# A reordered start in a fused attention and adapter kernel: VectorE only sums, idle matmuls, and a second group of queries loaded as fp32

## The chip, the cores and the metric

The kernel runs on one core of a Trainium2 chip. The core has five engines with instruction queues of their own: TensorE (PE: matmuls and transposes, with weight loads shown apart as PEld), VectorE (DVE), ScalarE (ACT), GpSimd (POOL) and SyncE (SP, which here only issues transfers). Sixteen DMA engines move data for all of them. An engine works through its queue in order, so an instruction that waits holds up all that stands behind it. The metric is the device time of one execution in microseconds (us), as a median over several runs; the profile comes from one execution by itself.

## The reference, cut to what matters

Two parts are fused. The first is attention with pooled keys: `kv` is averaged over 4x4 patches and multiplied by `w_sr`, and the result serves as keys and as values. The second is a mixture of small adapters on the attention's output, of which each row uses the best two of eight.

```python
# q: (4, 12288, 128), kv: (4, 384, 32, 128), w_sr: (128, 128), all fp32
kv_pool = kv.reshape(B, H // 4, 4, W // 4, 4, C).mean(axis=(2, 4))
k = v = kv_pool.reshape(B, -1, C) @ w_sr               # 768 keys per batch
s = (1 / sqrt(C)) * (q @ k.transpose(0, 2, 1))
s = s - s.max(-1, keepdims=True)
a = np.exp(s)
a /= a.sum(-1, keepdims=True) + 1e-09
x = (a @ v).reshape(B * N, C)                          # 49152 rows
logits = x @ w_gate                                    # 8 experts, rank 16 each
# the two largest logits of a row are kept, w = softmax over these two
out = x + sum over the two of w * ((x @ A[e]) @ B[e])
```

## The kernel before

The 49152 query rows are cut into 96 chunks of 512 (`NTOK`), 24 chunks to a batch, four chunks to a group of 2048 rows (`GROWS`, `GRP`). A batch has 768 keys, in six blocks of 128 (`NJ`), two blocks to one of three key tiles (`NT`). The order in which each engine gets its instructions is written out by hand, so the source is the order.

For a chunk `c` the work is: `scores(c, r)` (L231 to L240) for r = 0, 1, 2: two matmuls of a key tile's two blocks with the 512 queries into one of two PSUM buffers `sg`, and one exponential on ACT into `tt`, 1024 values per partition. `weigh(c, h)` (L242 to L251) for two halves: 12 matmuls each, with a piece of `tt` as weights and the values `vext` streaming, into the one buffer of `ps_x`. The values carry eight more columns for the gate's logits and one of ones for the softmax sum. `normalise(c)` (L253 to L267) on DVE: a reciprocal, a multiplication that frees `ps_x`, and four searches of the largest logits. `gate` and `gate_weights` on POOL, ACT and a little DVE, once for two chunks; `transposed` and its copy; `down`, `apply_gate`, `up` and `give` for the adapters, in chunks some iterations behind.

The main loop (L457 to L501) runs over c = 1 to 94. Iteration c computes scores for chunks c + 1 and c + 2, weighs and normalises chunk c - 1, transposes chunk c - 2, goes down with c - 3 and up with c - 6. From a list `todo` it takes three pieces of scores at set places of the iteration. The next batch's keys are prepared inside the loop by `prep` (L202 to L221): its `kv` tiles are loaded at k = 2, 6, 10 and summed on POOL at k = 5 to 15, where k is the chunk's place in its batch.

Queries reach `qT` (channels on partitions, bf16, one tile per group, three buffers) in two ways. Group 0 is loaded as fp32 into `q0` (L93, L97, four rows of 128 values for each of four chunks and each partition) and transposed on PE, in the first part of the program. Every other group goes through memory twice: `cast_q(g)` (L89 to L91) has POOL issue a transfer that turns 2048 rows into bf16 in `q_bf`, and `load_q(g)` (L227 to L229) has SP issue a transposing transfer from there.

The part ahead of the loop (L415 to L452) is what the change is about. SP loads the first batch's key tile 0, then `q0`, then key tiles 1 and 2, each in four transfers of 512 KB. For each key tile t, DVE adds four rows and then eight columns to pool (`sum_row`, L140, three of 1024 values, and `sum_cols`, L144 and L145); `tile_keys(t)` (L176 to L186) transposes the two blocks on PE into `ps_t`, copies them to `kpT` on DVE, multiplies by `w_sr` and copies to `kfT` on ACT; `tile_values(t)` (L188 to L194) makes the values, with the copy on ACT. `queries(h)` (L417 to L424) transposes two chunks of `q0` through `ps_x`, with the copies on ACT. Scores of chunks 0, 1 and 2 are put between. When the second rows of key tile 2 have landed, a small copy `tick` on POOL (L441) lets POOL issue the casts of groups 1, 2 and 3. `load_q(1)` and `load_q(2)` follow on SP.

`ps_x`, `ps_t` and `ps_h` hold one PSUM buffer each, `ps_s` two; `ttpool` has four buffers for `tt`. `mtile` takes the buffer of `ps_h`. `ranges(b)` (L196 to L200) are two DVE reductions over a batch's values for a check at the end.

The loop's lines for the scores and the weighing:

```python
        todo = [(c + 1, 2), (c + 2, 0), (c + 2, 1)]
        ...
        next_scores()
        if c >= 3 and c % 2 == 1:
            gate_weights((c - 3) // 2, nc.gpsimd)
        weigh(c - 1, 0)
        next_scores()
        ...
        weigh(c - 1, 1)
        normalise(c - 1)
```

Of the kernel before, what the change touches and what calls it, by code (L numbers as in the profile page):

```python
# [10 lines left out]
FP32 = mybir.dt.float32  # L11
BF16 = mybir.dt.bfloat16
# [9 lines left out]
def kernel(  # L22
# [10 lines left out]
    nc = tc.nc  # L33
# [55 lines left out]
    def cast_q(g):  # L89
        r = slice(g * GROWS, (g + 1) * GROWS)  # L90
        nc.gpsimd.dma_start(q_bf[r], qflat[r])  # L91

    q0 = kvpool.tile([P, GROWS // NTOK, NS, C], FP32, tag="kvt", name="q0")  # L93
    for t in range(NT):
        load_kv(0, t)
        if t == 0:
            nc.sync.dma_start(q0, qflat[0:GROWS].rearrange("(k s p) c -> p k s c", p=P, s=NS))  # L97

    w_in = const.tile([P, P], FP32)
    nc.scalar.dma_start(w_in, w_sr)  # L100
# [72 lines left out]
        nc.vector.tensor_copy(  # L173
            vext[b][:, :, 0:C + E].rearrange("p (h g) e -> p h g e", h=2), v)

    def tile_keys(t):  # L176

        k = slice(2 * t * P, 2 * (t + 1) * P)
        kp_ps = ps_t.tile([P, 2 * P], FP32, tag="tp", name="kp_ps")
        for u in range(2):  # L180
            mm(kp_ps[:, u * P:(u + 1) * P], kvt[0, t][:, 0, u, 0:C], id_f32, is_transpose=True,
               start=(u == 0), stop=(u == 1), skip_group_check=True)
        nc.vector.tensor_copy(kpT[0][:, k], kp_ps)
        k_ps = mtile([P, 2 * P], name="k_ps")
        mm(k_ps, w_sr_sb, kpT[0][:, k], start=True, stop=True)
        nc.scalar.activation(kfT[0][:, k], k_ps, AF.Copy)  # L186

    def tile_values(t):  # L188
        v_ps = mtile([P, 2, C + E], name="v_ps")
        for g in range(2):  # L190
            j = 2 * t + g
            mm(v_ps[:, g], kpT[0][:, j * P:(j + 1) * P], wext, start=(g == 0), stop=(g == 1),
               skip_group_check=True)
        nc.scalar.activation(vext[0][:, 2 * t:2 * t + 2, 0:C + E], v_ps, AF.Copy)  # L194

    def ranges(b):  # L196
        nc.vector.tensor_reduce(vmax[:, b:b + 1], vext[b][:, :, 0:C], axis=AX.XY,
# [33 lines left out]
    def scores(c, r):  # L231
        b = c // CPB
        if r == 0:
            tt[c] = ttpool.tile([P, NJ, NTOK], F16, tag="tt", name="tt")
        qc = qT[c // GRP][:, (c % GRP) * NTOK:(c % GRP + 1) * NTOK]
        sg = stile("sg")
        for k in range(2):
            j = 2 * r + k
            mm(sg[:, k], kfT[b][:, j * P:(j + 1) * P], qc, start=True, stop=True)  # L239
        nc.scalar.activation(tt[c][:, 2 * r:2 * r + 2], sg, AF.Exp, bias=0.0, scale=scale)  # L240

    def weigh(c, h):  # L242
        b = c // CPB
        if h == 0:
            xps[c] = ps_x.tile([P, 2, 512], FP32, tag="x", name="xps")
        for j in range(h * NH, (h + 1) * NH):
            for s in range(NS):
                o = xps[c][:, s // 2, (s % 2) * VW:(s % 2 + 1) * VW]
                mm(o, tt[c][:, j, s::NS], vext[b][:, j],  # L249
                   start=(j == 0 and s % 2 == 0), stop=(j == NJ - 1 and s % 2 == 1),  # L250
                   skip_group_check=True)  # L251

# [161 lines left out]

    qT[0] = qpool.tile([P, GROWS], BF16, tag="qT", name="qT")  # L415

    def queries(h):  # L417
        t = ps_x.tile([P, 2, NTOK], FP32, tag="x", name="q_ps")
        for u in range(2):
            k = 2 * h + u  # L420
            for i in range(NS):
                mm(t[:, u, i * P:(i + 1) * P], q0[:, k, i], id_f32, is_transpose=True,
                   start=(i == 0), stop=(i == NS - 1), skip_group_check=True)
            nc.scalar.activation(qT[0][:, k * NTOK:(k + 1) * NTOK], t[:, u], AF.Copy)  # L424

    a_bf = const.tile([P, P], BF16)
    b_half = const.tile([P, P], FP32)
    b_bf = const.tile([P, P], BF16)
    for t in range(NT):
        for d in range(1, 4):  # L430
            sum_row(0, t, d, nc.vector)
        sum_cols(0, t, nc.vector)
        tile_keys(t)
        if t == 0:
            nc.vector.tensor_copy(a_bf, a_f)
            nc.vector.tensor_scalar(b_half, b_f, 0.5, None, op0=ALU.mult)
            nc.vector.tensor_copy(b_bf, b_half)
            queries(0)
        if t == NT - 1:
            tick = const.tile([P, 1], FP32)  # L440
            nc.gpsimd.tensor_copy(tick, kvt[0, t][:, 1, 0, 0:1])  # L441
            for g in range(1, 4):
                cast_q(g)
        scores(0, t)
        tile_values(t)
        if t == 0:
            queries(1)
        scores(1, t)
        if t < NT - 1:
            scores(2, t)  # L450
    load_q(1)
    load_q(2)  # L452


# [2 lines left out]
    for c in range(1, NCH - 1):  # L457
        b, k = divmod(c, CPB)
        todo = [(c + 1, 2), (c + 2, 0), (c + 2, 1)]

        def next_scores():
            x, r = todo.pop(0)
            if x < NCH:
                scores(x, r)

        cs = c + 2
        if cs < NCH and cs % GRP == 0:
# [3 lines left out]
            if g + 3 < NQ:  # L471
                cast_q(g + 3)
        next_scores()
        if c >= 3 and c % 2 == 1:
            gate_weights((c - 3) // 2, nc.gpsimd)
        weigh(c - 1, 0)
        next_scores()
        if chunk_ok(c - 6):
            up(c - 6)
            give(c - 6)  # L480
        weigh(c - 1, 1)
        normalise(c - 1)
# [195 lines left out]
```

## Time and profile before

| What | us |
|---|---|
| median of three runs | 412.86 |
| lowest and highest of them | 411.19, 413.30 |
| the profiled execution | 412.09 |
| its span, first to last instruction | 410.3 |
| PE busy in the span | 380.0 (93%) |
| DVE busy | 344.4 (84%) |
| ACT busy | 297.9 (73%) |
| POOL busy | 165.2 (40%) |
| mean granted clock of PE | 0.991 |

The page's second part cuts the span into 40 equal slices of 10.26 us; each digit is an engine's busy share of a slice in tenths, 9 for 90% or more:

```profile
PE   0659999999999999999999999989999999999992
PEld 0426888777877888877877888867878788787791
DVE  3663789898899989898899989898898989899982
ACT  1267888876687877876687878866777888877751
POOL 1020498882212487792212488692212212122120
```

PE is busy almost throughout from the fourth slice on, which is the main loop. The first three slices, some 31 us, are the part ahead of the loop, where it is not. The last slice is the end of the work. A chunk's turn in the loop can be read from the start times of its reciprocal on DVE (L256), of which there are 96: the first at 36.1, the last at 395.0.

In the timeline a row gives the start and the duration of a group of like instructions, the engine, the line, the operation, what it writes and reads with partitions and elements, how many there are, and in brackets how long the engine had been idle before, and what ended that. In the windows view a row is a stretch of time with each engine's busy time in it, the clock granted to PE (PEclk, 1.00 is full), the busy share of the DMA engines and what they moved.

### The profile page before, as it was taken

Reading aid. Unit: us, or ns where it says so; the run is one execution under the profiler, and the core shown is the slowest. Engines: PE = TensorE matmul, PEld = TensorE weight load, DVE = VectorE, ACT = ScalarE, POOL = GpSimd, SP = SyncE. Lnnn points to the kernel's source line nnn. Section 1 sums busy time; section 2 is a strip of 40 time slices with the busy share of each in tenths; the row PEclk is TensorE's granted clock in tenths of the full one; section 3 lists DMA queues with packets and bytes.
Section 4 is the critical chain, followed back from the end, with each engine's and each line's share of the span. In section 5 each row is a group of like instructions: output and inputs, shape, how many; then the busy total and the mean of one; then the engine's idle time right before and its main releaser. Section 6 shows DMA issues by size and latency. Waiting matters only on the chain.

```text
span 410.3 us, 11470 instructions
## 1 busy us (share of the span) xinstructions
PE 380.0 (93%) x4561; PEld 304.0 (74%) x4561; DVE 344.4 (84%) x969; ACT 297.9 (73%) x356; POOL 165.2 (40%) x315
## 2 busy tenths in 40 slices
PE   0659999999999999999999999989999999999992
PEld 0426888777877888877877888867878788787791
DVE  3663789898899989898899989898898989899982
ACT  1267888876687877876687878866777888877751
POOL 1020498882212487792212488692212212122120
PEclk9998999999999999999999999999999999999998
DMA  8999699797186999797186999797185474221123
GB/s 259 378 251 181 232 248 289 284 185 154 66 169 134 290 244 310 241 249 156 60 173 119 322 233 305 263 227 154 55 180 115 139 162 129 79 78 74 57 80 135
DMA packets 71372, 76.51 MB, mean 186 GB/s; under 512 B 51744, under 2 KB 52000, under 8 KB 70944
## 3 DMA queue, kind: packets, MB, share of 16 engines
q1 hardware_dynamic: 68816, 62.93, 55.1%
q0 software_dynamic: 736, 12.06, 16.8%
q10 hardware_dynamic: 1760, 0.73, 0.7%
q8 instruction: 37, 0.61, 0.6%
q14 instruction: 23, 0.19, 0.1%
HBM read 50.53 MB, written 37.22 MB: 214 GB/s over the span
## 4 chain that ended last, share of the span: by engine, by line
PE 79%; DMA 8%; DVE 7%; issue 2%; ACT 1%; ACTq 0%; SPq 0%; DVEq 0%; POOL 0%
PE xps L249 31%; PE sg L239 26%; PE t_ps L306 9%; PE d_ps L350 5%; PE h_ps L329 4%; DMA qT<-q_bf 3%; DMA b_f<-in_moe_B_dram 3%; DMA kvt<-in_kv_dram 2%; DVE xn L260 2%; DVE hg L334 2%; DMA q_bf<-in_q_dram 1%; PE v_ps L171 1%; PE k_ps L164 1%; DVE osb L358 1%; ACT tt L240 1%
## 5 line engine op out<-in xcount | busy, mean ns | idle before, releaser
L240 ACT ACTIVATE tt<-sg 128x1024 f16<-128x1024 f32 x288 | 282.6, 1022 | 75.8 <-PE sg L239 75.3
L239 PE MATMUL sg<-qT,kfT 128*128 128x512 bf16 x576 | 172.3, 382 | 2.4 <-ACT kfT L186 1.0
L249 PEld LDWEIGHTS <-tt 128*128 128x128 f16 x2304 | 154.6, 113 | 23.7 <-DVE xn L260 2.1
L249 PE MATMUL xps<-vext,tt 128*128 128x137 f16 x2304 | 170.9, 224 | 0.6 <-DVE xn L260 0.4
L358 DVE TENSOR_TENSOR osb<-d_ps,xn 128x512 f32<-128x512 f32 x90 | 62.1, 689 | 17.7 <-PE d_ps L350 14.3
L273 POOL TENSOR_TENSOR m<-top 128x8 f32<-128x8 f32 x47 | 10.9, 232 | 157.5 <-DVE top L267 157.2
L260 DVE TENSOR_TENSOR xn<-xps,rinv_all 128x548 f32<-128x548 f32 x96 | 69.9, 728 | 3.3
L140 POOL TENSOR_TENSOR kvt<-kvt 128x1024 f32<-128x1024 f32 x27 | 64.0, 2372 | 4.3 <-PE sg L239 1.9
L334 DVE TENSOR_TENSOR hg<-h_ps,gw 128x512 bf16<-128x512 f32 x94 | 63.8, 678 | 0.4 <-PE h_ps L329 0.4
L315 DVE COPY xh<-t_ps 128x1024 bf16<-128x1024 bf16 (+1 forms) x93 | 62.4, 671 | 0.0
L239 PEld LDWEIGHTS <-kfT 128*128 128x128 bf16 x576 | 45.3, 98 | 5.7 <-issue 2.3
L350 PEld LDWEIGHTS <-xh 128*128 128x128 bf16 x384 | 29.2, 98 | 25.8 <-issue 5.6
L329 PEld LDWEIGHTS <-xh 128*128 128x128 bf16 x384 | 29.2, 98 | 21.0 <-issue 0.7
L267 DVE MAX8 top<-xn 128x8 f32<-128x8 f32 x384 | 36.0, 156 | 3.3
L350 PE MATMUL d_ps<-b_bf,xh 128*128 128x128 bf16 x360 | 34.8, 219 | 3.2 <-DVE hg L334 2.9
L329 PE MATMUL h_ps<-a_bf,xh 128*128 128x128 bf16 x376 | 36.3, 219 | 0.6 <-DVE cnt L398 0.6
L306 PE MATMUL t_ps<-id_bf,hg 128*128 128x128 bf16 x376 | 36.3, 219 | 0.0
L306 PE MATMUL t_ps<-id_bf,xn 128*128 128x128 bf16 x376 | 36.3, 219 | 0.0
L288 POOL TENSOR_SCALAR th<-th 128x64 f32<-128x64 f32 x47 | 17.4, 370 | 37.4 <-ACT th L286 37.4
L256 DVE RECIPROCAL rinv_all<-xps 128x4 f32<-128x4 f32 x96 | 17.5, 183 | 14.4 <-PE xps L249 11.5
L306 PEld LDWEIGHTS <-xn 128*128 128x128 bf16 x384 | 26.0, 98 | 0.0
L306 PEld LDWEIGHTS <-hg 128*128 128x128 bf16 x384 | 25.4, 98 | 0.1
(96 smaller groups left out, 207.4 us busy)
## 6 DMA issues: line engine op xcount, KB each, us to landing
kvt<-in_kv_dram SPq DMA_DIRECT2D x48, 512.0 KB, 7.2
out_dram<-osb SPq DMA_DIRECT2D x94, 256.0 KB, 3.0
q_bf<-in_q_dram POOLq DMA_DIRECT2D x23, 512.0 KB, 6.3
out_dram<-osb ACTq DMA_DIRECT2D x2, 256.0 KB, 3.7
qT<-q_bf SPq DMA_TRANSPOSE x23, 6.7
w_in<-in_w_sr_dram ACTq DMA_DIRECT2D x1, 64.0 KB, 2.0
a_f<-in_moe_A_dram ACTq DMA_DIRECT2D x1, 64.0 KB, 9.6
b_f<-in_moe_B_dram ACTq DMA_DIRECT2D x1, 64.0 KB, 10.3
```

The source lines that it names most:

```text
L140: eng.tensor_tensor(v[:, 0], v[:, 0], v[:, d], op=ALU.add)
L239: mm(sg[:, k], kfT[b][:, j * P:(j + 1) * P], qc, start=True, stop=True)
L240: nc.scalar.activation(tt[c][:, 2 * r:2 * r + 2], sg, AF.Exp, bias=0.0, scale=scale)
L249: mm(o, tt[c][:, j, s::NS], vext[b][:, j], start=(j == 0 and s % 2 == 0), stop=(j == NJ - 1 and s % 2 == 1), skip_group_check=True)
L260: nc.vector.tensor_tensor(xn[c].rearrange("p (b s) v -> p b s v", b=2), xv, ri.rearrange("p (b s) -> p b s", b=2).unsqueeze(3).broadcast_t ...
L267: nc.vector.max(gin[c // 2][:, (c % 2) * NS + s], xn[c][:, s, C:C + E])
L306: mm(t_ps[:, k, s], src, id_bf, is_transpose=True, start=(i == 0), stop=(i == len(todo) - 1), skip_group_check=True)
L315: nc.vector.tensor_copy(xh[:, lo:hi_], t_ps[:, lo:hi_])
L329: mm(hps[c][:, s], xT[c][:, s], a_bf, start=(s == 0), stop=(s == NS - 1))
L334: nc.vector.tensor_tensor(hg[c].rearrange("p s (e r) -> p (s e) r", r=RK), hps[c].rearrange("p s (e r) -> p (s e) r", r=RK), g.rearrange(" ...
L350: mm(dps[c][:, s], hgT[c][:, s], b_bf, start=(s == 0 and not plus_x), stop=(s == NS - 1), skip_group_check=True)
L358: nc.vector.tensor_tensor(osb, dps[c], xn[c][:, :, 0:C], op=ALU.add)
```

## The change

It touches the part ahead of the loop and the first iterations.

- The second group of queries, rows 2048 to 4095, is loaded as fp32 into a new tile `q1`, by one more SP transfer behind all key loads. `queries_1(k)` transposes chunk 4 + k on PE through `ps_t`, and DVE copies it to `qT[1]`. `cast_q(1)` and `load_q(1)` go.
- In `q0` and `q1` a partition now holds four neighbouring rows of a chunk, 2 KB in one piece, where `q0` had four pieces of 512 bytes. So in the first eight chunks a column block of `tt` is a run of 128 columns, where it was every fourth column, and `weigh` slices accordingly.
- DVE's queue has all sums of the three key tiles first. `kpT` of key tiles 0 and 1 is copied by ACT; the values of key tile 2 are copied by DVE.
- `queries(k)` now does one chunk at a time in half the buffer's size, four calls, put between other work.
- `warm(count)` issues matmuls of the bf16 identity with itself, 128x512 each, into the buffer of `ps_h`; nothing reads them. There are 18 ahead of key tile 0, 8 and 2 around key tile 1, and 2 ahead of key tile 2.
- Chunk 0 is weighed and normalised ahead of the loop, and `scores(3, 0)` is made there; iteration 1 has two pieces of scores left and no weighing.
- `tick` waits for `q1` instead of key tile 2; the casts of groups 2 and 3 follow it.
- `ranges(0)` moves from iteration 1 to iteration 10.

```diff
+    q1 = kvpool.tile([P, GROWS // NTOK, NS, C], FP32, tag="q1", name="q1", bufs=1)
     q0 = kvpool.tile([P, GROWS // NTOK, NS, C], FP32, tag="kvt", name="q0")
     for t in range(NT):
         load_kv(0, t)
         if t == 0:
-            nc.sync.dma_start(q0, qflat[0:GROWS].rearrange("(k s p) c -> p k s c", p=P, s=NS))
+            nc.sync.dma_start(q0, qflat[0:GROWS].rearrange("(k p s) c -> p k s c", p=P, s=NS))
+    nc.sync.dma_start(q1, qflat[GROWS:2 * GROWS].rearrange("(k p s) c -> p k s c", p=P, s=NS))
...
-    def tile_keys(t):
+    def tile_keys(t, between=lambda: None):
...
-        nc.vector.tensor_copy(kpT[0][:, k], kp_ps)
+        if t < NT - 1:
+            nc.scalar.activation(kpT[0][:, k], kp_ps, AF.Copy)
+        else:
+            nc.vector.tensor_copy(kpT[0][:, k], kp_ps)
+        between()
...
-        nc.scalar.activation(vext[0][:, 2 * t:2 * t + 2, 0:C + E], v_ps, AF.Copy)
+        if t < NT - 1:
+            nc.scalar.activation(vext[0][:, 2 * t:2 * t + 2, 0:C + E], v_ps, AF.Copy)
+        else:
+            nc.vector.tensor_copy(vext[0][:, 2 * t:2 * t + 2, 0:C + E], v_ps)
...
-                mm(o, tt[c][:, j, s::NS], vext[b][:, j],
+                rows = slice(s * P, (s + 1) * P) if c < 2 * GRP else slice(s, NTOK, NS)
+                mm(o, tt[c][:, j, rows], vext[b][:, j],
...
-    def queries(h):
-        t = ps_x.tile([P, 2, NTOK], FP32, tag="x", name="q_ps")
-        for u in range(2):
-            k = 2 * h + u
-            for i in range(NS):
-                mm(t[:, u, i * P:(i + 1) * P], q0[:, k, i], id_f32, is_transpose=True,
-                   start=(i == 0), stop=(i == NS - 1), skip_group_check=True)
-            nc.scalar.activation(qT[0][:, k * NTOK:(k + 1) * NTOK], t[:, u], AF.Copy)
+    def queries(k):
+        t = ps_x.tile([P, NTOK], FP32, tag="x", name="q_ps")
+        for i in range(NS):
+            mm(t[:, i * P:(i + 1) * P], q0[:, k, i], id_f32, is_transpose=True,
+               start=(i == 0), stop=(i == NS - 1), skip_group_check=True)
+        nc.scalar.activation(qT[0][:, k * NTOK:(k + 1) * NTOK], t, AF.Copy)
+
+    qT[1] = qpool.tile([P, GROWS], BF16, tag="qT", name="qT")
+
+    def queries_1(k):
+        t = ps_t.tile([P, NTOK], FP32, tag="tp", name="q_ps")
+        for i in range(NS):
+            mm(t[:, i * P:(i + 1) * P], q1[:, k, i], id_f32, is_transpose=True,
+               start=(i == 0), stop=(i == NS - 1), skip_group_check=True)
+        nc.vector.tensor_copy(qT[1][:, k * NTOK:(k + 1) * NTOK], t)
+
+    def warm(count):
+
+        t = mtile([P, NS, P], name="w_ps")
+        for i in range(count):
+            mm(t, id_bf, id_bf.unsqueeze(1).broadcast_to([P, NS, P]), start=True, stop=True)
...
+    tick = const.tile([P, 1], FP32)
+    nc.gpsimd.tensor_copy(tick, q1[:, 0, 0, 0:1])
+    cast_q(2)
+    cast_q(3)
     for t in range(NT):
         for d in range(1, 4):
             sum_row(0, t, d, nc.vector)
         sum_cols(0, t, nc.vector)
-        tile_keys(t)
         if t == 0:
             nc.vector.tensor_copy(a_bf, a_f)
             nc.vector.tensor_scalar(b_half, b_f, 0.5, None, op0=ALU.mult)
             nc.vector.tensor_copy(b_bf, b_half)
-            queries(0)
-        if t == NT - 1:
-            tick = const.tile([P, 1], FP32)
-            nc.gpsimd.tensor_copy(tick, kvt[0, t][:, 1, 0, 0:1])
-            for g in range(1, 4):
-                cast_q(g)
-        scores(0, t)
-        tile_values(t)
-        if t == 0:
-            queries(1)
-        scores(1, t)
-        if t < NT - 1:
-            scores(2, t)
-    load_q(1)
+    warm(18)
+    tile_keys(0, lambda: queries(0))
+    queries(1)
+    scores(0, 0)
+    tile_values(0)
+    queries(2)
+    scores(1, 0)
+    queries(3)
+    scores(2, 0)
+    scores(3, 0)
+    warm(8)
+    tile_keys(1)
+    warm(2)
+    scores(0, 1)
+    tile_values(1)
+    scores(1, 1)
+    weigh(0, 0)
+    warm(2)
+    tile_keys(2)
+    scores(0, 2)
+    tile_values(2)
+    queries_1(0)
+    scores(2, 1)
+    scores(1, 2)
+    weigh(0, 1)
+    normalise(0)
+    queries_1(1)
     load_q(2)
...
         todo = [(c + 1, 2), (c + 2, 0), (c + 2, 1)]
+        if c == 1:
+            todo = [(2, 2), (3, 1)]
...
         next_scores()
+        if c < 3:
+            queries_1(c + 1)
...
-        weigh(c - 1, 0)
+        if c > 1:
+            weigh(c - 1, 0)
...
-        weigh(c - 1, 1)
-        normalise(c - 1)
+        if c > 1:
+            weigh(c - 1, 1)
+        if c > 1:
+            normalise(c - 1)
...
-        if c == 1:
+        if c == 10:
             ranges(0)
```

More of the change, by code (lines that the diff above doesn't have):

```diff
@@ L459 @@
         todo = [(c + 1, 2), (c + 2, 0), (c + 2, 1)]
+        if c == 1:
+            todo = [(2, 2), (3, 1)]
         def next_scores():
-            x, r = todo.pop(0)
-            if x < NCH:
-                scores(x, r)
+            if todo:
+                x, r = todo.pop(0)
+                if x < NCH:
+                    scores(x, r)
         cs = c + 2
```

## The prediction, made before the changed kernel had run

> **What bounds the kernel now.** Three views, in this order: the windows table over the first 38 us, the timeline of the same stretch, and two pieces of the timeline around 113 us. Times are microseconds from the span's start; "chunk" is 512 queries, and a chunk is dated by its reciprocal (L256).
>
> ```profile
> core 0: us, PE busy (x) PEld busy (x) DVE busy (x) ACT busy (x) POOL busy (x), PEclk, DMA share, GB/s
> 10.00:14.00 4.00, 0.69 (x2) 0.29 (x2) 2.94 (x6) 0.00 (x0) 0.00 (x0) 1.00 1.05 322
> 14.00:17.00 3.00, 2.26 (x7) 1.57 (x8) 1.00 (x5) 0.98 (x2) 0.00 (x0) 1.00 1.03 412
> 17.00:20.50 3.50, 3.50 (x14) 2.72 (x13) 3.36 (x4) 1.92 (x3) 0.00 (x0) 1.00 1.02 406
> 20.50:24.00 3.50, 2.30 (x13) 1.36 (x12) 1.92 (x4) 2.67 (x4) 2.38 (x5) 1.00 1.52 431
> 24.00:27.30 3.30, 2.29 (x11) 1.04 (x10) 3.20 (x4) 2.60 (x5) 0.00 (x0) 1.00 0.81 169
> 27.30:30.70 3.40, 1.28 (x5) 0.61 (x6) 1.37 (x3) 1.56 (x3) 0.00 (x0) 1.00 0.75 154
> 30.70:34.10 3.40, 3.40 (x14) 2.09 (x13) 0.00 (x0) 2.31 (x4) 0.00 (x0) 0.52 0.86 181
> ```
>
> Two things are to be seen. From 10 to 14 us, while q0 is on its way, the DMA moves 322 GB/s; afterwards it moves 406 to 412. And TensorE's clock falls to 0.52 in the stretch after the one in which PE was busy only 1.28 of 3.40 us; it stayed whole after stretches with 2.30 of 3.50 and 2.29 of 3.30. (Before 20.5 us the column shows 1.00, but the rows run at half rate: two 128x512 matmuls at 17.73 take 1.06 us, and 0.59 at 24.69.)
>
> ```profile
> 16.50 3.79 DVE L140 TENSOR_TENSOR kvt<-kvt 128x1024 f32<-128x1024 f32 x3 [1.97 <-DMA kvt<-in_kv_dram]
> ...
> 23.01 0.42 DVE L183 COPY kpT<-kp_ps 128x256 f32<-128x256 f32 x1 [1.54 <-PE kp_ps L181]
> 23.35 3.73 DVE L140 TENSOR_TENSOR kvt<-kvt 128x1024 f32<-128x1024 f32 x3
> ...
> 28.33 0.44 PE L181 MATMUL kp_ps<-id_f,kvt 128*128 128x128 f32 x2 [1.33 <-DVE kvt L145]
> ...
> 36.05 0.18 DVE L256 RECIPROCAL rinv_all<-xps 128x4 f32<-128x4 f32 x1 [6.82 <-PE xps L249]
> ...
> 38.49 0.60 PE L239 MATMUL sg<-qT,kfT 128*128 128x512 bf16 x2 [0.52 <-DMA qT<-q_bf]
> ...
> 39.86 0.18 DVE L256 RECIPROCAL rinv_all<-xps 128x4 f32<-128x4 f32 x1 [1.50 <-PE xps L249]
> ```
>
> DVE sits idle for 1.54 us, copies kpT, and only then sums the third key tile; PE waits for that sum until 28.33. Chunk 0 ends at 36.05, chunk 1 at 39.86, after a wait for qT. From there the chunks follow at 3.12, 3.19, 3.42 and then 3.64 us with PE continuously busy. So whatever the change gains before 39.86 moves everything behind it, and a gain that is used up before chunk 1 is lost.
>
> ```profile
> 112.89 0.93 DVE L197 TENSOR_REDUCE vmax<-vext 128x1 f32<-128x768 f16 x1
> 113.75 0.19 DVE L199 TENSOR_REDUCE vmax<-vext 128x1 f32<-128x48 f16 x1
> 113.86 0.68 DVE L334 TENSOR_TENSOR hg<-h_ps,gw 128x512 bf16<-128x512 f32 x1
> ```
> ```profile
> 114.59 0.38 PE L350 MATMUL d_ps<-b_bf,xh 128*128 128x128 bf16 x4 [0.31 <-DVE hg L334]
> ```
>
> This is ranges() inside the steady part: hg starts 0.97 us late, PE then waits.
>
> **The change, step by step.** *q0 in longer pieces.* The DMA view has q0 in pieces of 0.5 KB, landing 9.9 us after 3.93, so at 13.83; the last load of tile 0 landed at 10.3. That is 3.5 us for 1 MB. The loads of tiles 1 and 2 land 1.25 us apart for half as much, so 2.5 us per MB in 4 KB pieces; the new 2 KB pieces lie between. Gain 0 (the small loads on ACT's queue, which land at 12.5, are the brake) to 1.0 us; I take 0.5. The Trainium skill, "DMA: Bandwidth & Descriptors", section Specifications, puts full rate at 512 bytes and up, which speaks against a gain; by it the ramp gains 1.0 and the sum would be 411.8. The row of 322 against 412 GB/s leans the other way.
>
> *DVE only sums.* Tile 1's first sum starts at 16.0 instead of 16.50, its sums end at 20.9 (4.96 us from first to last, as from 16.50 to 21.46). Tile 2's three loads land at 21.5, 22.8 and 24.0 (issues 13.72, 14.37, 15.01 and 7.8, 8.4, 9.0 us to landing), less 0.5. Three sums of 1.23, the last from 23.6, then 0.69 and 0.42: done at 26.0 instead of 28.28. The copy of 0.42 is now on ACT (0.39 to 0.40 us by the kfT row) and is queued there behind exponentials of 1.02.
>
> *PE's own queue takes some of it back.* With the clock whole, PE starts scores(3,0) at 19.6: its three predecessors on ACT are two exponentials and the four qT copies of 0.60. Behind it are 8 idle matmuls, 8 x 0.216 (half the spacing of a pair) = 1.73 us, to 21.74, so tile 1's transposes start 0.8 us after their data. From there: copy on ACT to 22.6, keys 0.70, kfT to 23.8, two idle matmuls 0.43, scores(0,1) at 24.3, its exponential 24.9 to 25.9, vext for tile 1 behind it to 26.3, the last 4 matmuls of weigh(0,0) after that, two more idle matmuls, and tile 2's transposes at 27.0. The data was there at 26.0, so the start is 1.3 us earlier than 28.33, not 2.3. Idle matmuls ahead of all this (18 from 6.2 us) cost 18 x 0.216 to 18 x 0.43, ending between 10.1 and 13.9; tile 0's sums end at 12.8, so 0 to 1.1 us late, hidden by the wait for tile 1's loads unless the 13.9 comes true (then the ramp loses 0.5).
>
> *To chunk 1.* Transposes, DVE copy, keys, kfT, scores, exponential: 2.77 us at full clock against 28.33 to 31.35 before. Then on PE: scores 0.43, values 0.47, four transposes of q1 0.50 (their row at 21.23), two scores 0.86, weigh 0.73, so chunk 0's reciprocal comes at 32.3, 3.7 us earlier. But PE must also transpose the other three quarters of q1, each through the one buffer of ps_t. The DVE copy has no row of its own; 128x256 takes 0.425 and 128x768 0.958, so 128x512 takes 0.69. Below that bound is ACT's 0.60, above it 0.96; I take 0.69. The chain: reciprocal, xn and max 1.27 us to 33.6, copy to 34.3, transposes 0.65, copy to 35.7, transposes to 36.3, weigh 0.73, scores 0.43, weigh 0.73 and 0.2 to the result: chunk 1 at 38.35. That is 1.5 us before 39.86. The wait of 0.52 for qT is inside this, and so is what replaces it: PE now waits some 1.3 us for DVE's copies.
>
> *ranges at c == 10.* At 37.32 it cost nothing: DVE waited 1.50 us afterwards. In the steady part it delays hg by 0.97. At c == 21 this cost 0.48 (4.12 against 3.64). At an even c the gate's mask comes ahead of hg, and hg ended at 62.72 with PE's use at 63.00, 0.28 spare: 0.97 - 0.28 = 0.7. Bounds 0.3 and 1.0; I take 0.7.
>
> *DMAs moved.* One 1 MB load joins SP's queue behind the 8 key loads (landing 24.0 - 0.5 + 2.5 = 26.0; first needed at 30.0). One cast and one transpose of group 1 go. The casts of groups 2 and 3, and that of group 4 behind them on POOL, now wait for q1: 26.0 instead of 21.58. The next transpose waits on SP for the first of them, 26.0 + 5.8 = 31.8, and behind it stand the transpose of group 3, and batch 1's first key loads, at 40.44 before. Taking 7.3 us for the first transpose and 2.75 for the second as before, the loads go out at 41.9, and their second lands 5.8 later, near 48.3. POOL wants it at 49.95 - 1.5 = 48.45. Cost 0 to 1.0; I take 0, hidden by POOL's own wait for ACT.
>
> Contiguous instead of strided weights in weigh for 8 chunks: nothing, since a weight load (113 ns, overlapping) ends before its matmul's turn.
>
> Sum: -1.5 + 0.7 = -0.8. The profiled execution took 412.09 (span 410.3 and 1.8 around it), which gives 411.3. It lies 0.77 below the median 412.86 of runs that spread over 2.1 us; from the median it would be 412.1. I name 411.7, the middle. What can be told from no change is about 0.5%, 2.06 us.
>
> **The rivals.** *The clock falls in the new prologue* (the slower side). By my walk PE's queue is occupied 53 to 60% in each 3.4 us between 16 and 30; counted alike, the old stretch 24.0 to 27.3 was 52% and kept the clock, 27.3 to 30.7 was 26% and lost it. The limit lies between. If some stretch falls below it at 24 to 30, scores, values, transposes and weigh to chunk 0 run at half rate, 2.6 us more at most, 2.2 after what ACT's exponentials hide: 411.3 + 2.2 = 413.5, and with two such stretches 415.7. It decides from 1.5 us of loss in the ramp on. The Trainium skill, "TensorE: Matmul & The Clock Gate", Part 1, takes the clock back only after an idle window of about 3.4 us; no gap here is that long, and by that rule this rival is dead. But 27.3 to 30.7 held five matmul rows and the clock fell all the same, so the row decides. The same page's Part 4 says that transposes do not count as busy, which speaks against leaning on the query transposes; no row here separates them.
>
> *POOL's late key loads go away.* At chunks 38 and 62 the spacing is 4.36 and 5.18 instead of 3.64: POOL's sum waits 1.1 and 1.9 us for loads, and hg waits for POOL's gate. If the shift of the queues removes both, 2.26 more is gained: 409.0. For it: only a queue's phase makes them. Against: SP's order from c == 2 on is unchanged.
>
> *The ramp gains more*: q0 a full 1.0, weigh(0,0) not held by vext: -2.5 + 0.7, 410.3.
>
> *Batch 1's loads come late at c == 5* by the 1.0 above: 412.3.
>
> **How the numbers follow.** Forecast 0.48, clock 0.20, POOL's waits gone 0.13, larger ramp 0.10, late loads 0.09. The forecast's own range is 410.6 to 412.8. The 8 in 10 reach down to 409.5, leaving out most of the third case's lower half, and up to 414.2, leaving out the upper half of the clock case. Faster than 410.8: 0.11 of the POOL case, 0.06 of the larger ramp, 0.07 of the forecast's lower edge and the spread of runs, 0.24. Slower than 414.9: half of the clock case, 0.10, and 0.02. The rest, 0.64, is within.
>
> **What would show it.** Tile 2's sums end near 26.0 and its transposes start near 27.0; chunk 0's reciprocal near 32.3, chunk 1's near 38.4, with PE waiting for DVE's qT copies between; granted clock 1.00 from 14 to 38; spacing at chunk 10 of 4.3. A clock of 0.5 anywhere from 20 to 34, or chunk 1 later than 39.9, would prove the forecast wrong; so would a chunk 1 before 37.

## The result and the profile after

The changed kernel took 409.25 us (median of 7 runs, 407.56 to 411.19) beside 411.95 for the kernel before (7 runs, 410.52 to 413.30): a ratio of 0.994, with a 95% interval of 0.9918 to 0.9963 (such intervals stand in brackets below). It is faster by 0.6%, a little more than the 0.5% that can be told, and by more than was predicted. The median of the kernel before had come down from 412.86 with three runs to 411.95 with seven.

The profiled execution took 410.03 (span 408.2), against 412.09 (410.3). The windows view of the changed kernel, in the same stretches as before:

```profile
core 0: us, PE busy (x) PEld busy (x) DVE busy (x) ACT busy (x) POOL busy (x), PEclk, DMA share, GB/s
10.00:14.00 4.00, 3.41 (x19) 1.57 (x16) 3.28 (x7) 0.38 (x1) 0.00 (x0) 1.00 1.05 410
14.00:17.00 3.00, 2.87 (x19) 2.01 (x18) 0.97 (x1) 2.48 (x5) 0.00 (x0) 1.00 1.04 406
17.00:20.50 3.50, 2.58 (x13) 1.26 (x13) 3.37 (x4) 3.50 (x6) 0.00 (x0) 1.00 1.00 400
20.50:24.00 3.50, 2.55 (x12) 1.26 (x11) 3.21 (x5) 1.26 (x3) 0.00 (x0) 1.00 1.03 400
24.00:27.30 3.30, 2.85 (x24) 1.96 (x22) 2.43 (x4) 2.23 (x3) 1.03 (x3) 1.00 0.35 127
27.30:30.70 3.40, 2.84 (x16) 1.88 (x17) 1.06 (x3) 1.57 (x3) 0.86 (x2) 1.00 0.89 154
30.70:34.10 3.40, 2.23 (x24) 1.66 (x22) 1.97 (x8) 2.80 (x3) 0.00 (x0) 1.00 1.42 299
```

From 10 to 14 us the DMA moves 410 GB/s, where it moved 322. The clock is 1.00 throughout: the dip to 0.52 at 30.7 is gone. The timeline of the changed kernel:

```profile
16.03 3.77 DVE L143 TENSOR_TENSOR kvt<-kvt 128x1024 f32<-128x1024 f32 x3 [2.53 <-DMA kvt<-in_kv_dram]
...
19.64 1.89 PE L448 MATMUL w_ps<-id_bf 128*128 128x512 bf16 x8
...
21.14 3.79 DVE L143 TENSOR_TENSOR kvt<-kvt 128x1024 f32<-128x1024 f32 x3
...
21.37 0.38 PE L184 MATMUL kp_ps<-id_f,kvt 128*128 128x128 f32 x2
...
25.68 0.42 DVE L148 TENSOR_TENSOR kvt<-kvt 128x256 f32<-128x256 f32 x1
...
26.49 0.38 PE L184 MATMUL kp_ps<-id_f,kvt 128*128 128x128 f32 x2
...
31.69 0.18 DVE L267 RECIPROCAL rinv_all<-xps 128x4 f32<-128x4 f32 x1 [0.90 <-PE xps L260]
...
32.97 0.67 DVE L442 CAST qT<-q_ps 128x512 bf16<-128x512 f32 x1
...
33.70 0.66 PE L440 MATMUL q_ps<-id_f,q 128*128 128x128 f32 x4 [1.17 <-DVE qT L442]
...
37.71 0.18 DVE L267 RECIPROCAL rinv_all<-xps 128x4 f32<-128x4 f32 x1 [1.19 <-PE xps L260]
```

DVE starts tile 2's sums 0.2 us after tile 1's, at 21.14 instead of 23.35; PE takes up tile 2 at 26.49 instead of 28.33. Chunk 0 ends at 31.69 (36.05 before), 4.4 us earlier, but chunk 1 only 2.15 us earlier (37.71 against 39.86): PE waits at 33.70 for DVE to empty the one buffer of the query transposes. From chunk 1 to chunk 9 the difference stays between 2.15 and 2.17, so the changed column blocks of the first eight chunks cost or bring nothing. At chunk 10 it falls to 1.42, from ranges(), whose row stands here with the PE wait behind it:

```profile
67.16 0.94 DVE L207 TENSOR_REDUCE vmax<-vext 128x1 f32<-128x768 f16 x1
...
68.86 0.38 PE L361 MATMUL d_ps<-b_bf,xh 128*128 128x128 bf16 x4 [0.58 <-DVE hg L345]
```

Chunk 10's spacing is 4.39 us instead of 3.64. The later long spacings, where POOL's sums wait for key loads, add 1.98 over the usual ones, against 2.39 before. The last chunk is at 393.17 instead of 394.99, 1.82 earlier, and the time is 2.06 less: another 0.24 lies behind the last chunk.

### The profile page after: what moved, and what is told of

The parts are those of the page before. It is cut to its first block, busy times and chain, and to the rows that moved or that the text cites. A ratio compares the mean times of both kernels' runs of the same rounds, so it can differ in the third digit from the quotient of the medians.

```text
span 408.2 us, 11562 instructions
## 1 busy us (share of the span) xinstructions
PE 385.4 (94%) x4607; PEld 306.0 (75%) x4607; DVE 346.5 (85%) x972; ACT 298.2 (73%) x357; POOL 164.6 (40%) x314
## 4 chain that ended last, share of the span: by engine, by line
PE 82%; DVE 10%; ACT 2%; issue 2%; DMA 2%; SPq 0%; DVEq 0%
PE xps L260 32%; PE sg L249 27%; PE t_ps L317 9%; PE d_ps L361 5%; PE h_ps L340 4%; DVE xn L271 2%; DVE hg L345 2%; DMA kvt<-in_kv_dram 2%; ACT tt L250 1%; PE v_ps L174 1%; DVE top L278 1%; PE k_ps L167 1%; DVE vmax L207 1%; DVE osb L369 1%; DVE xh L326 1%
```

## Experiments

Each kernel is an edit of the changed one unless named otherwise, and its ratio is to the kernel before, run beside it. Four figures are read from each trace: the first sum of tile 1 on DVE ("first sum"), chunk 1, the last chunk, and the "late loads", that is what the spacings above the usual ones add where POOL waits for keys. To hold a kernel's start against its repeats, the unchanged programs were traced again too.

**ranges() back at c == 1** (`e1_ranges_1`).

```diff
-        if c == 10:
+        if c == 1:
             ranges(0)
```

> The changed kernel with ranges(0) back in iteration 1. Theory: in iteration 10 the two reductions hold up hg by 0.97 us and PE waits 0.6 for it, so chunk 10 follows chunk 9 by 4.39 instead of 3.64; in iteration 1 they fall between DVE's copies of the third and fourth quarter of q1, and DVE was idle for 1.19 us ahead of chunk 1's reciprocal. Expected: chunk 10's spacing 3.64, chunk 1's reciprocal still within 0.1 of 37.7, and 0.74 us less time. Rival: the copy of q1's last quarter starts 0.3 us later behind the reductions, PE's next use of the ps_t buffer waits, and the ramp gives back half or more: chunk 1 at 38.1 or later and the time the same within 0.3 us.

Chunk 1 at 37.41, 22.0 after the first sum of 15.40; chunk 10's spacing 3.64; last chunk 390.95. Median 408.76 (10 runs), ratio 0.995 [0.9918, 0.9981]. The 0.75 us at chunk 10 come back. Chunk 1 comes 0.3 later against the first sum than in the changed kernel, but that 0.3 is there at chunk 0 already, ahead of the reductions (31.39, 15.99 after the first sum, against 15.66), and from chunk 0 to chunk 1 both take 6.02. So at c == 1 the reductions cost nothing that the trace shows. The ratios, 0.995 and 0.994, do not resolve a gain of this size.

**Key loads one iteration earlier**, in the changed kernel (`e2_loads_early`) and in the kernel before (`e3_before_loads_early`).

```diff
-        if k in (2, 6, 10):
-            load_kv(b, (k - 2) // 4)
+        if k in (1, 5, 9):
+            load_kv(b, (k - 1) // 4)
```

> The changed kernel with the key loads of the next batch issued one iteration earlier (k = 1, 5, 9 instead of 2, 6, 10), so that on SP's queue they stand ahead of a group's transposing transfer and not behind it. Theory: the spacings above 3.64 at chunks 34, 58 and 62 (4.00, 4.75, 4.15) come from POOL's sums waiting for these loads; with them landing one chunk earlier the spacings there go to 3.64, which is 1.98 us less in the profiled execution, and the runs spread over less than the 3.6 us between 407.56 and 411.19. Rival: the loads only take their wait to another transfer (the transposes behind them come late instead, or the sums still wait because the DMA engines are the limit): chunks with spacings of 4 and more remain, and the median stays within 0.7 us of 409.25.

> The kernel before with the same one edit to its key loads. Theory: it loses its 0.13, 0.72 and 1.54 us at chunks 34, 38 and 62, so some 2.4 us below 411.95 at most and 1.5 in the median; the distance to the changed kernel with the same edit is then the ramp and ranges alone, 2.15 - 0.74 + 0.3 at the end = 1.7 us. Rival, that the changed kernel is faster in good part because its later loads happen to be less late: the distance between the two falls below 1.0 us.

Slower: 418.19 (4 runs), ratio 1.0164 [1.0107, 1.0220], and 418.96 (three runs; a fourth, of 429.94, is left out), 1.0192 [1.0090, 1.0295]. The late loads grow to 10.3 and 8.6 us. My theory was wrong. From the timeline of the first:

```profile
77.83 7.20 SPq L239 DMA_TRANSPOSE qT<-q_bf  x1
...
82.79 4.82 POOL L143 TENSOR_TENSOR kvt<-kvt 128x1024 f32<-128x1024 f32 x2 [3.61 <-DMA kvt<-in_kv_dram]
...
90.17 0.69 DVE L345 TENSOR_TENSOR hg<-h_ps,gw 128x512 bf16<-128x512 f32 x1 [1.77 <-POOL gw L300]
```

One transposing transfer occupies SP's queue for 7.2 us here, POOL waits 3.6 us for keys, and DVE 1.8 us for POOL's gate behind them. The order of loads and transposing transfers on SP's queue is worth several times the change under study. The pair was meant to say which kernel is nearer to a late load; with more late loads on both sides it does not.

**No idle matmuls** (`e4_no_idle_matmuls`) and **only the first 18** (`e11_only_18`).

```diff
-    warm(18)
...
-    warm(8)
...
-    warm(2)
...
-    warm(2)
```

> The changed kernel without any of its 30 idle matmuls. Theory: they keep the clock; without them PE is occupied for less than half of the stretches around 21 to 27 us and starts its work at 13 us at half rate, so rows of two 128x512 score matmuls show 1.06 us instead of 0.59 from 13 to 20 us and again somewhere from 24 to 34, and chunk 1's reciprocal comes 1 to 2 us later than 37.71, at 38.7 to 39.7. Rival: the real work keeps the clock by itself and the idle matmuls only stand in PE's way (tile 1's transposes 0.4 us and tile 2's 0.4 us late): chunk 1 at 37.3 and the time 0.4 us less.

> The changed kernel with the 18 idle matmuls at the start alone, the other 12 removed. Theory: the 12 hold the clock between 20 and 28 us; without them it falls somewhere from 20.5 to 34 as it did without any (0.52 from 24.0 to 27.3), tile 1's matmuls run at half rate, and chunk 1 comes 0.4 to 0.8 later against tile 1's first sum, 22.1 to 22.5 after it. Rival: the clock, once up, is kept by the real work (PE occupied in 1.9 of 3.5 us), the 12 only stand in the way, and chunk 1 comes 21.1 to 21.4 us after the first sum.

Without any, the windows view of the first shows

```profile
20.50:24.00 3.50, 1.92 (x9) 1.08 (x9) 3.23 (x3) 2.01 (x5) 0.00 (x0) 0.96 1.03 397
24.00:27.30 3.30, 3.30 (x20) 2.41 (x19) 1.56 (x3) 2.26 (x3) 1.48 (x4) 0.52 0.26 96
```

and of the second

```profile
20.50:24.00 3.50, 1.26 (x5) 0.61 (x6) 2.92 (x5) 1.56 (x3) 0.00 (x0) 1.00 1.02 410
24.00:27.30 3.30, 3.30 (x19) 2.50 (x18) 3.03 (x4) 2.26 (x3) 0.00 (x0) 0.54 0.71 272
```

The clock falls to 0.52 and 0.54 in the stretch after the thin one, exactly where the changed kernel holds 1.00 with 2.55 of 3.50 us busy. Chunk 1 comes 22.68 and 22.44 us after the first sum, against 21.68 in the changed kernel. In the second, DVE paused twice for loads and began tile 2's sums 5.83 after tile 1's instead of 5.11, which accounts for nearly all of it. So all the idle matmuls together are worth 1.0 us of ramp, by the first trace. Its loads flowed (411, 408 and 397 GB/s between 14 and 24 us), and in nine other traces with flowing loads and all the idle matmuls (after, e1, e2, e5, e6, e7, e8, e10, e12) the clock kept 1.00 through the ramp. What the 12 between the key tiles are worth alone stays open: the clock fell without them in e11, but there the DMA moved only 320 and 303 GB/s from 14 to 20.5 us, and under such loads it also fell with all of them in place (e15 and e16, below). The times do not resolve it: 409.57 and 409.29 (10 runs each), ratios 0.9946 [0.9914, 0.9977] and 0.9934 [0.9909, 0.9960].

**Group 1 through memory again** (`e5_group1_cast`, and `e16_group1_cast_2` as a second trace). The cast and the transposing transfer of group 1 replace q1 and its PE transposes; the rest of the change stays, but for the row order of chunks 4 to 7, which goes back with it.

```diff
-    q1 = kvpool.tile([P, GROWS // NTOK, NS, C], FP32, tag="q1", name="q1", bufs=1)
...
-    nc.gpsimd.tensor_copy(tick, q1[:, 0, 0, 0:1])
+    nc.gpsimd.tensor_copy(tick, kvt[0, NT - 1][:, 1, 0, 0:1])
+    cast_q(1)
...
-    queries_1(1)
+    load_q(1)
```

> The changed kernel with group 1 again by a cast and a transposing transfer (no q1, no queries_1, tick on key tile 2, casts of groups 1 to 3), the rest of the reordering kept. Theory: chunk 0 comes as early as in the changed kernel or 0.5 us earlier (no q1 transposes ahead of it, 31.2 to 31.7), but PE then waits for the transfer, which lands at 38.4 as in the kernel before, so that the scores of chunk 4 start at 38.4 and chunk 1 ends at 39.8: all of the 2.16 us in the ramp hangs on q1. Rival: the casts start at 21.5 with less in their way, the transfer lands by 36.5, and chunk 1 comes at 37.5 to 38.0: q1 is worth nothing by itself.

> The version with group 1 by a cast and a transposing transfer, a second trace. Its first had chunk 1 at 37.68, as early as the changed kernel, while its median is 2 us above. Theory: in most executions the transfer lands later than the 36.2 of that trace, and chunk 1 comes at 38.3 or later, over 22.7 us after the first sum. Rival: it repeats (22.5 after the first sum), and the 2 us come from behind chunk 1: late key loads of over 2.5 us, or a spacing that the changed kernel doesn't show.

The first trace, in its timeline:

```profile
30.79 0.18 DVE L265 RECIPROCAL rinv_all<-xps 128x4 f32<-128x4 f32 x1 [1.52 <-PE xps L258]
...
36.31 0.60 PE L247 MATMUL sg<-qT,kfT 128*128 128x512 bf16 x2 [2.69 <-DMA qT<-q_bf]
37.68 0.18 DVE L265 RECIPROCAL rinv_all<-xps 128x4 f32<-128x4 f32 x1 [5.53 <-PE xps L258]
```

The second, at the same wait:

```profile
38.40 0.60 PE L247 MATMUL sg<-qT,kfT 128*128 128x512 bf16 x2 [1.59 <-DMA qT<-q_bf]
```

In the first, chunk 0 is done at 30.79, but PE waits 2.69 us for qT, and chunk 1 is at 37.68, level with the changed kernel: the rival's numbers, not my theory's. It had an early start, though. Its first sum is at 15.16, and from there to chunk 1 it takes 22.52 us, 0.84 more than the changed kernel. In the second trace the wait ends at 38.40 and chunk 1 is at 39.77, 23.9 after its first sum. That trace is no clean repeat: its loads moved 300 and 368 GB/s between 14 and 20.5 us, the clock was 0.51 from 24.0 to 27.3, and chunk 0 came only at 33.99. The median of the kernel is 411.30 (10 runs) against 412.31, ratio 0.999 [0.9963, 1.0016]. So with group 1 through memory a faster chunk 0 is used up by the transfer's landing; q1 takes that out. Of the edits that undo one part it is the only one whose interval holds 1. The landing follows the loads: in the six traces in which PE waits for it (before, e3, e5, e9, e14, e16) the wait ends 15.9 to 17.5 us after the start of `tick`, which waits for key tile 2. The kernel before with q1 alone was not run.

**q0 in 512 byte pieces** (`e6_q0_512`), with the strided rows in `weigh` for group 0 that go with it.

```diff
-            nc.sync.dma_start(q0, qflat[0:GROWS].rearrange("(k p s) c -> p k s c", p=P, s=NS))
+            nc.sync.dma_start(q0, qflat[0:GROWS].rearrange("(k s p) c -> p k s c", p=P, s=NS))
```

> The changed kernel with q0 loaded in pieces of 512 bytes as before (and strided weights in weigh for chunks 0 to 3). Theory: the pieces slow the loads, the DMA moves 320 to 330 GB/s from 10 to 14 us instead of 410, tile 1's first sum starts 0.5 us later than 16.03, at 16.5, and chunk 1 ends 0.5 us later, at 38.2. Rival: ACT's small loads in the same stretch were the brake in the kernel before, and the first sum stays within 0.15 us of 16.03.

Its windows view and its timeline:

```profile
10.00:14.00 4.00, 2.91 (x13) 1.13 (x11) 2.83 (x6) 0.38 (x1) 0.00 (x0) 1.00 1.06 315
```
```profile
16.65 3.78 DVE L143 TENSOR_TENSOR kvt<-kvt 128x1024 f32<-128x1024 f32 x3 [2.46 <-DMA kvt<-in_kv_dram]
```

From 10 to 14 us the DMA moves 315 GB/s again, with everything else as in the changed kernel, and the first sum is at 16.65, 0.62 later; chunk 1 is at 38.34, 21.69 after it. Over the traces of all kernels the DMA moved 315 to 325 GB/s from 10 to 14 us in the six with 512 byte pieces, and 398 to 413 in the twelve with 2 KB. The first sum over the traces of all kernels, by q0's layout: with 512 bytes 16.16, 16.18, 16.46, 16.50, 16.65, 17.82; with 2 KB 15.16, 15.25, 15.29, 15.33, 15.40, 15.53, 15.70, 15.85, 15.97, 16.03, 16.36, 16.72. The medians are 16.48 and 15.6, 0.9 us apart, though the two sets overlap, and five of the first six are kernels with the old order. The time was 409.53 (10 runs), ratio 0.9935 [0.9912, 0.9957]: such a difference is within the spread.

**The copy of kpT on DVE**, between the sums of two tiles (`e7_kpT_on_dve`): each tile's sums move to just ahead of its `tile_keys`.

```diff
-        if t < NT - 1:
-            nc.scalar.activation(kpT[0][:, k], kp_ps, AF.Copy)
-        else:
-            nc.vector.tensor_copy(kpT[0][:, k], kp_ps)
+        nc.vector.tensor_copy(kpT[0][:, k], kp_ps)
```

> The changed kernel with kpT of all key tiles copied by DVE between the sums, as before, and everything else as changed. Theory: DVE stands idle from 21.0 until tile 1's transposes are done at 21.75, copies for 0.42, and tile 2's sums end 1.1 us later, near 27.2 instead of 26.1; of these PE's queue hides the 0.39 by which it is late for tile 2 in the changed kernel, so chunk 1 comes 0.7 us later, at 38.4. Rival: PE's queue is the limit between 21 and 27 us, not DVE's, and chunk 1 stays within 0.2 us of 37.7.

Tile 2's sums start at 21.85, 6.15 after tile 1's (5.11 in the changed kernel), and chunk 1 comes 22.40 after the first sum instead of 21.68: "DVE only sums" is worth 0.72 us with the rest in place. Of the 1.0 us by which DVE is freed, PE's queue keeps 0.3. Time 410.20 (10 runs), ratio 0.9956 [0.9924, 0.9989].

**A second buffer for the query transposes**, with ranges() at c == 1 (`e8_two_buffers`), and with the next batch's first key loads one iteration earlier on top (`e12_two_buffers_load`; the last hunk is this one's alone).

```diff
-        t = ps_t.tile([P, NTOK], FP32, tag="tp", name="q_ps")
+        t = (mtile([P, NTOK], name="q_ps") if k % 2 else
+             ps_t.tile([P, NTOK], FP32, tag="tp", name="q_ps"))
...
-        if k in (2, 6, 10):
-            load_kv(b, (k - 2) // 4)
+        if k in ((1, 6, 10) if b == 1 else (2, 6, 10)):
+            load_kv(b, (k - 1) // 4)
```

> A version meant to be faster: ranges(0) in iteration 1, and the odd quarters of q1 transposed through the buffer of ps_h, so that PE need not wait for DVE's copy of the quarter before. Theory: the wait of 1.17 us at 33.7 goes and the one at 35.1 with it, PE's own work sets chunk 1, which comes at 36.5 to 36.8 instead of 37.7, and chunk 10 follows at 3.64: 1.7 us less than the changed kernel apart from late key loads. Rival: ACT's exponentials, which are 11 us of work ahead of chunk 1, take the wait's place, and chunk 1 comes no earlier than 37.3.

> The version with ranges(0) in iteration 1 and q1's odd quarters through ps_h, with batch 1's first key loads issued one iteration earlier, so ahead of group 3's transposing transfer on SP. Theory: in the version without this POOL waited 1.22 us for these loads at 46.1, and chunk 6 came 1.02 late; now chunk 6 follows at 3.64, chunk 1 comes 20.6 to 20.7 us after tile 1's first sum, and the time is 1 us below the version without it and 2.5 to 3 below the changed kernel apart from later key loads. Rival: as when all key loads were issued earlier, the transfer behind them comes late instead, and a wait of 1 us or more appears before chunk 20.

The first, in its timeline:

```profile
32.34 1.27 DVE L443 CAST qT<-q_ps 128x512 bf16<-128x512 f32 x2
...
35.97 0.18 DVE L267 RECIPROCAL rinv_all<-xps 128x4 f32<-128x4 f32 x1 [0.79 <-PE xps L260]
...
47.30 4.80 POOL L143 TENSOR_TENSOR kvt<-kvt 128x1024 f32<-128x1024 f32 x2 [1.22 <-PE sg L249]
```

Chunk 1 comes 20.64 after the first sum, 1.04 sooner, so PE's waits for DVE's copies cost a microsecond. But now batch 1's loads bind: POOL stands idle for 1.22 us ahead of its sum at c == 5, and chunk 6 takes 1.02 longer. The profile names PE as what ended that wait; moving only the loads takes it away, so it was the loads: in the second kernel the sum starts at 45.93 with no idle time shown, and chunk 6 is at the usual 3.64. The times are 407.54 (4 runs), ratio 0.9878 [0.9820, 0.9937], and 407.09 (5 runs, 406.64 to 407.89), 0.9908 [0.9878, 0.9939]. The second has the lowest median found, 2.1 us below the changed kernel's 409.15, run beside it; their intervals overlap, so the two cannot be told apart by time. In e12 the spacing at chunk 14 was 0.59 over the usual one: less than the rival's 1 us, but some of the wait may have moved there.

**The unchanged programs again**: the kernel before (`e9_before_again`, `e13_before_3`, `e14_before_4`) and the changed one (`e10_after_again`, `e15_after_3`).

> The kernel before once more, for a second trace of it. Open is why the medians lie 2.7 us apart where the chunks of the two traces account for 2.16 (ramp) - 0.75 (ranges) + 0.41 (late key loads) + 0.25 (end). Theory: in the kernel before chunk 1 hangs on the transposing transfer of group 1, whose landing differs from one execution to the next, so chunk 1 comes at 39.9 to 41 here, at least 0.3 later than 39.86, and the late key loads at chunks 34 to 62 sum to something other than 2.39. Rival: the ramp repeats to within 0.2 us (chunk 1 at 39.7 to 40.0), and only the late key loads differ between executions.

> The changed kernel once more. Theory: chunk 1 depends on no transfer but the key loads and repeats relative to tile 1's first sum (21.68 us after it), chunk 10's spacing is 4.39 again, and what differs is the first sum itself (15.2 to 16.1 in the runs so far) and the late key loads at chunks 14 to 62 (0.8 to 2.7 us). The ratio to the kernel before comes out at 0.992 to 0.996. Rival: chunk 1 shifts by over 0.3 us against the first sum because the clock falls in some executions.

> The kernel before, a third trace. Theory: the trace that the forecast was made from was a quick one at the start; tile 1's first sum lies between 16.4 and 18 us, chunk 1 23.3 to 24.5 us after it (39.8 to 42.4), the scatter after the first sum being the wait for group 1's transposing transfer. Rival: 17.82 and 42.17 of the second trace were an outlier, and this one repeats the first within 0.3 us (16.5 and 39.9).

> The kernel before, a fourth trace, with the expectation of the third: theory, first sum 16.4 to 18 us and chunk 1 between 40.2 and 42.4 in at least one of the two; rival, both within 0.3 us of 39.9.

> The changed kernel, a third trace. Theory: first sum 15.2 to 16.4, chunk 1 21.6 to 22.0 us after it (36.8 to 38.4), so that the means of the ramps of the two kernels lie about 3 us apart and not 2.16. Rival: chunk 1 scatters as widely as in the kernel before, by 2 us, and the two traces so far were quick ones.

| Trace | first sum | chunk 1 | last chunk | late loads | its time |
|---|---|---|---|---|---|
| before | 16.50 | 39.86 | 394.99 | 2.39 | 412.09 |
| e9 (before) | 17.82 | 42.17 | 396.09 | 1.21 | 413.31 |
| e13 (before) | 16.18 | 40.12 | 393.69 | 0.81 | 410.83 |
| e14 (before) | 16.16 | 39.96 | 395.24 | 2.52 | 412.32 |
| after | 16.03 | 37.71 | 393.17 | 1.98 | 410.03 |
| e10 (after) | 15.25 | 36.98 | 390.46 | 0 | 407.34 |
| e15 (after) | 16.72 | 42.27 | 396.43 | 0.67 | 413.59 |

e10 was also timed: 409.15 (10 runs), ratio 0.9953 [0.9929, 0.9976]. The same program differs in where chunk 1 lies, by 2.3 us (before) and 5.3 (after), and in the late loads by 1.7 and 2.0. My expectation for e13 and e14 missed in part: chunk 1 came 23.9 and 23.8 after the first sum, as expected, but both first sums came before 16.4, and chunk 1 lies within 0.3 of the first trace, as the rival had it. So 42.17 in e9 is the exception. For e15 the rival came true as well. In the kernel before, PE's wait for qT at the end of the ramp, 0.52 in the trace that I predicted from, was 1.62 in e9, 1.55 in e14 and absent in e13. In e9 the first loads were slow (291 and 301 GB/s from 14 to 20.5 us), and pairs of 128x512 matmuls still took 1.03 us at 27.64, the half rate that the first trace had left by 24.69. The changed kernel can start badly too, as the windows view of e15 shows:

```profile
14.00:17.00 3.00, 2.75 (x19) 2.20 (x20) 0.97 (x4) 2.18 (x5) 0.00 (x0) 1.00 0.57 168
...
20.50:24.00 3.50, 1.53 (x8) 0.48 (x5) 2.01 (x3) 1.00 (x2) 0.00 (x0) 1.00 0.99 385
24.00:27.30 3.30, 1.96 (x8) 1.06 (x9) 3.09 (x4) 0.77 (x2) 0.00 (x0) 0.98 1.02 407
27.30:30.70 3.40, 3.40 (x20) 2.67 (x20) 2.04 (x3) 2.34 (x3) 1.16 (x3) 0.52 0.25 93
```

Its loads ran at 168 GB/s from 14 to 17 us instead of 406, DVE's third sum of tile 1 came at 21.93, PE had too little to do, and the clock fell to 0.52 in spite of the idle matmuls. Chunk 1 came 25.55 after the first sum.

## Why the prediction was wrong, step by step

The direction and the mechanisms held. The step that failed is the ramp's term: -1.5 was forecast, and the two profiled executions show -2.15. That alone would have left the result inside the range. From the trace that I worked from, 412.09 less 2.15 (ramp), plus 0.74 (ranges), less 0.41 (late loads) and less 0.24 (behind the last chunk) is 410.03, the changed kernel's profiled execution. The last two I had at nothing, the late loads as a rival. The median lies 0.78 lower still, and I had named 411.7 where my sum gave 411.3. So 409.25 came out below the 409.5 that the range reached down to by a ramp term too small, by the choice of 411.7 and by scatter between executions; no trace shows another mechanism.

*q0 in longer pieces*: taken as 0.5, measured 0.47 in the first pair of traces, 0.62 by e6 and 0.9 between the medians of the first sums, all inside its bounds of 0 to 1.0. By the Trainium skill, "DMA: Bandwidth & Descriptors", section Specifications, pieces of 512 bytes should already run at the full rate; 315 to 325 against 398 to 413 GB/s in the same stretch say otherwise here, though small loads on ACT's queue lie beside both.

*DVE only sums, and PE's own queue takes some of it back*: the right mechanism. The sums of tile 2 ended at 26.10 (25.68 and 0.42 long) where I had 26.0, and PE's queue did hold the transposes back, to 26.49 and not to 27.0. PE was at scores(3,0) at 19.21 instead of 19.6, and the copy to vext started at 25.38 instead of 25.9.

*To chunk 1*: this is the term that was mis-sized. From the first sum to chunk 1 my walk has 22.35 us; the changed kernel needs 21.7 (after, e2, e6, e10) to 22.0 (e1) where the loads flow. Chunk 1 came at 37.71 instead of 38.35. Of these 0.64, 0.51 were there when tile 2's transposes started, from the two starts above, and another 0.10 at chunk 0 (31.69 instead of 32.3); the rest of the walk held. The copy at 0.69 was as priced, and PE's wait behind it was 1.17 where I had 1.3; two buffers in place of one gained 1.04.

*What it was held against*: the ramp of one trace. Over five traces with the old prologue (e3's among them, at 40.40) chunk 1's median is 40.12, and the 39.86 that I subtracted from is the earliest of them. Over the five traces with the new prologue as it is (after, e1, e2, e10 and e15) it is 37.64, so the ramp gains some 2.5 us by the medians, 2.1 by the means (e15 is among the five), 2.15 in the first pair of traces, and not 1.5. The base itself explains little of it: only e9 lies over 0.6 from 39.86.

*ranges at c == 10*: 0.7 predicted, 0.75 measured, and given back by e1. *DMAs moved*: no cost, as taken: POOL's sum at c == 5 started at 47.78 without a wait. *Clock*: 1.00 from 14 to 38, and e4, where the loads flowed and it fell, shows that the idle matmuls hold it where the loads flow.

*The rivals.* The clock case fell in the first trace and came true in e15, where slow first loads starved PE; its line between a stretch that keeps the clock and one that loses it was drawn by PE's share alone, and that does not hold (last section). The larger ramp was the right one in kind: 2.1 to 2.5, against its 2.5. Late loads at c == 5 cost nothing until the ramp was shortened further (e8). POOL's late key loads did not vanish; they vary from 0 to 2.5 us in traces of the same programs.

*The sum.* 2.5 of ramp less 0.75 is 1.75, and the medians differ by 2.70, with 1.5 to 3.4 by the interval: 1.75 is inside it. What fills the remaining 0.9 stays open; the late loads, 0 to 2.5 us per trace on either side, are more than large enough, but four traces and three do not show a difference. That the first pair's late loads and end went the same way as the change, by 0.65, looks like chance. I also named the middle between the profiled execution's scale and the median of three runs; the first, 411.3, was nearer.

Which part brings the time? Taking q1 back left 0.999; taking back the 512 byte pieces, the DVE order or the idle matmuls left 0.9935 to 0.9956, each with an interval below 1. In the traces each of these three is worth 0.6 to 1.0 us of ramp, which the medians, 0.3 to 0.95 above the changed kernel's, do not resolve. With 2.05 for q1 (411.30 against 409.25) the losses one by one add to more than the 2.70 of the whole, so the parts seem not to be additive: as long as group 1's transfer lands last, as in before, e3, e5, e9, e14 and e16, what the others gain ends in a wait for it. That this holds in most executions the traces suggest and do not settle.

## What to carry to other kernels

Freeing the engine that is late pays only up to the next queue: here PE's own instructions kept 0.3 of 1.0 us, one staging buffer between PE and DVE another 1.0, and a transfer that landed late, in one trace after a wait of 2.69 us, could use up the whole. A reduction that nobody waits for belongs where its engine idles; inside this saturated loop it cost 0.75 of its 1.05 us. Take several traces of the kernel before as well: a start that varies by 2 us hides a change of that size, and one trace may hold a mild case of the very wait that the change removes (0.52 us here, 1.55 and 1.62 in two others, none in a third).

## What the runs showed of the hardware

The clock falls without an idle window. PE was busy 1.92 of 3.50 us (e4), 1.26 of 3.50 (e11), 1.28 of 3.40 (before), 1.98 of 3.50 (e16), and 1.53 of 3.50 and then 1.96 of 3.30 (e15), and in the stretch after each (in e15, after the second) the granted clock was 0.51 to 0.54; it held after 2.30 of 3.50 and 2.29 of 3.30 (before) and after 2.55 of 3.50 (after). The Trainium skill, "TensorE: Matmul & The Clock Gate", Part 1, takes the clock back after an idle window of about 3.4 us, but also tells of a kernel in which frequent short idle times were enough. The longest idle time of PE around these stretches is 2.4 us (e15, ahead of 24.39), so in these runs a part-filled stretch was enough. PE's busy share in such a stretch does not decide it, though. In e5 PE waited 2.69 us for qT and was busy for less time than in the stretch of the kernel before:

```profile
34.10:37.50 3.40, 1.19 (x15) 0.96 (x16) 0.00 (x0) 0.48 (x1) 0.00 (x0) 1.00 1.18 240
```

The clock stayed at 1.00 there and in the 3.4 us from 38.0 on. Where a stretch is cut changes the share (in e5 1.68 of 3.40 us from 31.5, 1.94 from 34.9). What decides stays open; no run was made for it.

The first loads do not always flow. Between 14 and 20.5 us the DMA moved 397 to 412 GB/s in 14 of the 18 traces, but 291 and then 301 in e9 (14 to 17, 17 to 20.5), 320 and 303 in e11, 300 and 368 in e16, and 168 and 276 in e15. What else was under way in the chip then, no trace shows; it was not settled.
